# Paired score products on two row groups, with decode and scaling moved between engines, in a fused attention and feed-forward kernel

## The chip, the cores and the metric

The kernel runs on one core of one Trainium2 chip. The metric is the device time of one execution in microseconds; the median of the runs counts.

## The reference, cut to what matters

Windowed attention with a linear bias per head, then two feed-forward blocks over the same 2304 tokens. Sizes: 4 batches, 8 heads, 576 positions, head size 64, window 128.

```python
scores = scale * np.matmul(q, k.transpose(0, 1, 3, 2))
mask = (rel >= 0) & (rel < window)
scores = np.where(mask, scores + bias[None], -1000000000.0)
attn = np.exp(scores - np.max(scores, axis=-1, keepdims=True))
attn = attn / (np.sum(attn, axis=-1, keepdims=True) + 1e-09)
x = np.matmul(attn, v)                     # (B, H, S, D), reshaped to (2304, 512)
h = x @ w_in                               # (2304, 2048)
g = s * np.maximum(h, 0.0) ** 2 + b
x = g @ w_out                              # (2304, 512)
out = ((x @ w1) * (x @ w2)) @ w3 @ w_out2  # the second block
```

The six weight matrices arrive as eight-byte floats; the kernel turns them into single precision itself ("decode").

## The kernel before, in words

The 2304 tokens are cut into six tiles of 384 (`TT`), each of three blocks of 128 queries. A block looks at its own 128 keys and the 128 before them. Attention goes tile by tile, head by head: the heads of tile 0 come first and alone, the heads of tile t+1 are laid between the chunks of the feed-forward work of tile t. A time-line simulation at build time orders each engine's instructions; those passed to `keep_in_program_order` stay in the order in which the code issues them.

The change is about tile 0, whose eight heads (`EARLY`, g = 0 to 7) form four pairs. I call this part the front. Two heads of a pair share one q tile and one k tile, head 0 on partitions 0 to 63, head 1 on 64 to 127. Each call of `slot(n, ...)` (line 1099) for n = 0 to 7 issues for its head:

- `att_scores` (294): first `keep_active` (76), products of zeros that are not used: ten ahead of head 0, two ahead of each other head. Then three products (305), one for each query block, with 64 contracted rows, into two PSUM tiles of the pool `ps_rot`.
- `att_min` (314): VectorE adds the distance table to the three blocks and takes the minimum of each row (324).
- `att_transpose` and `att_select` of the head before: TensorE transposes five 128x128 blocks (380), ScalarE copies them out (394, 395).
- `att_exp` (336): ScalarE, three exponentials (341).
- `tick` (202), as often as `dec` says, for n = 0 to 7: 1, 1, 2, 1, 2, 2, 1, 0 times. A tick starts one decode of a 128x512 weight chunk and finishes the one before. `decode` (89) starts with z on ScalarE (102): the upper half of each number, strided by two, times 2^-112. The rest is VectorE: a shift of z (104), and two operations that combine z and the raw chunk (107, 113). The tile z has two buffers. Raw chunks are loaded on SP's queue (84), three ahead of need.
- `att_v` (409) and `att_x` (446) of the head two before: TensorE multiplies by V with a column of ones (420). After the second head of a pair VectorE forms 1/(sum+1e-9) (452, 455) and multiplies the whole 128x384 product by it (457). TensorE transposes that (462), and `att_xt` (474) copies it out on ScalarE (480). This is a quarter of the input `xT` of tile 0's first product `hp` (505).

After n = 7, `flush` (1082) does what is left of heads 6 and 7. Then slots n = 8 on lay tile 1's heads (310, 311, 272, 257, 347) between the chunks of tile 0's feed-forward block (`hp` 505, `acc` 560), and the decodes go on there.

Of the kernel before, what the change touches and what calls it, by code (L numbers as in the profile page):

```python
# [8 lines left out]
F32 = mybir.dt.float32  # L9
# [3 lines left out]
AF = mybir.ActivationFunctionType  # L13
ALU = mybir.AluOpType

B, H, S, D = 4, 8, 576, 64
# [5 lines left out]
P = 128  # L22
TT = 384
NTILE = NT // TT
NB = TT // P
# [7 lines left out]
EARLY = H  # L33
# [7 lines left out]
def kernel(  # L41
    ctx: ExitStack, tc: tile.TileContext, qk0, qk, v, relm, w_in, w_out, s, b, w1, w2, w3T, wo2, v0, out
):
    nc = tc.nc
# [9 lines left out]
    ps_acc = ctx.enter_context(tc.tile_pool(name="ps_acc", bufs=4, space=PSUM))  # L54
# [21 lines left out]
    def keep_active(dst, n):  # L76
        for _ in range(n):
            nc.tensor.matmul(
                out=dst, lhsT=zeros[:, :P], rhs=zeros[:, :dst.free_size()], start=True, stop=True
            )  # L80
# [8 lines left out]
    def decode(raw, pool, tag, done, free=None, plain=False):  # L89

        z = zp.tile([P, DM], F32, tag="z", name="z")
        pin = tc.keep_in_program_order if pinned[0] else lambda i: i
        if raw.dtype == F32:
            nc.vector.tensor_copy(out=z, in_=raw)
            yield
        else:
            zu = z.bitcast(U32)
            wu = raw.bitcast(U32).rearrange("p (n t) -> p n t", t=2)  # L100
            wf = raw.bitcast(F32).rearrange("p (n t) -> p n t", t=2)
            pin(nc.scalar.activation(out=z, in_=wf[:, :, 1], func=AF.Copy, scale=2.0 ** -112))
            yield
            pin(nc.vector.tensor_scalar(
                out=zu, in0=zu, scalar1=3, scalar2=None, op0=ALU.logical_shift_left
            ))
            pin(nc.vector.scalar_tensor_tensor(
                out=zu, in0=wu[:, :, 1], scalar=0x80000000, in1=zu,
                op0=ALU.bitwise_and, op1=ALU.bitwise_or,
            ))  # L110
            if plain:
                z = pool.tile([P, DM], F32, tag=tag, name="wz")
            nc.vector.scalar_tensor_tensor(
                out=z.bitcast(U32), in0=wu[:, :, 0], scalar=29, in1=zu,
                op0=ALU.logical_shift_right, op1=ALU.bitwise_or,
            )
            if plain:
                done(z)
                yield
                return  # L120
        if free:
            free()
        yield
        w = pool.tile([P, 2, DM], F32R, tag=tag, name="w")
        nc.scalar.activation(out=w[:, 0, :], in_=z, func=AF.Copy)
        nc.gpsimd.tensor_tensor(
            out=w[:, 1, :], in0=z, in1=w[:, 0, :].bitcast(F32), op=ALU.subtract
        )
        done(w)
        yield  # L130
# [59 lines left out]
                    npre[0] += 1  # L190
                    next(p[1])

    pinned = [False]
    flight, todo, keep, raws, nraw, need = [], [], [True], [], [0], [0]

    def load_raws(n):
# [17 lines left out]
    qkraw, vraw, qa, ka, kb, vv, ns, pr, mins, sums, tps, pt, xf, xT, xo = ({} for _ in range(15))  # L214
# [77 lines left out]
        vv[g // 2] = x  # L292

    def att_scores(g):
        a, k, kl = qa.pop(g), ka.pop(g), kb.pop(g, None)
        s0 = ps_rot.tile([P, 2, 2 * P], F32, tag="rot", name="s0")
        s1 = ps_rot.tile([P, 2, 2 * P], F32, tag="rot", name="s1")
        dst = [s0[:, 0, :], s0[:, 1, :], s1[:, 0, :]]
        if g < EARLY:
            keep_active(s0.rearrange("p n q -> p (n q)"), 2 if g else 10)  # L300
        for i in range(NB):
            qs, ks = slice(i * P, (i + 1) * P), slice(i * P, (i + 2) * P)
            if g < EARLY:
                hs, c0 = slice(g % 2 * D, (g % 2 + 1) * D), P if i == 0 else 0
                nc.tensor.matmul(
                    out=dst[i][:, c0:], lhsT=a[hs, qs], rhs=k[hs, i * P + c0:(i + 2) * P],
                    start=True, stop=True,
                )
                continue
            nc.tensor.matmul(out=dst[i], lhsT=a[:, qs], rhs=k[:, ks], start=True, stop=False)  # L310
            nc.tensor.matmul(out=dst[i], lhsT=a[:, qs], rhs=kl[:, ks], start=False, stop=True)  # L311
        ns[g] = dst

    def att_min(g):
        t, h = divmod(g, H)
# [129 lines left out]
    def att_x(g):  # L445
        t, h = divmod(g, H)
        p, e = divmod(g, 2)
        if g < EARLY:
            if e:
                acc = xo.pop(p)  # L450
                rs = ep.tile([P, NB, 2, 1], F32, tag="sm", name="rs")
                nc.vector.tensor_scalar(
                    out=rs, in0=acc[:, :, :, D:], scalar1=1e-9, scalar2=None, op0=ALU.add
                )
                nc.vector.reciprocal(out=rs, in_=rs)
                xs = ap.tile([P, NB, 2, D], F32, tag="cs", name="xs")
                nc.vector.tensor_tensor(
                    out=xs, in0=acc[:, :, :, :D], in1=rs.to_broadcast([P, NB, 2, D]), op=ALU.mult
                )
                xf[p] = ps_acc.tile([P, TT], F32, tag="acc", name="xt")  # L460
                for i in range(NB):
                    nc.tensor.transpose(
                        xf[p][:, i * P:(i + 1) * P], xs[:, i].rearrange("p e d -> p (e d)"), ident
                    )
            return
        pv = tps.pop((g, 0))
        if e == 0:
            xf[p] = ap.tile([P, TT], F32, tag="xf", name="xf")
        main, corr = (slice(0, D), slice(D, P)) if e == 0 else (slice(D, P), slice(0, D))
        cs = ap.tile([P, TT], F32, tag="cs", name="cs")  # L470
        nc.scalar.activation(out=cs[main, :], in_=pv[corr, :], func=AF.Copy)
        nc.vector.tensor_tensor(out=xf[p][main, :], in0=pv[main, :], in1=cs[main, :], op=ALU.add)
# [582 lines left out]
    for c in range(NC1):  # L1055
        for d, src in ((wi, w_in[c]), (wo, w_out[c * P:(c + 1) * P, :])):
            raw = wp.tile([P, DM], src.dtype, tag="w", name="raw")
            raws.append((raw, src))
            todo.append(
                lambda raw=raw, d=d, c=c: decode(  # L1060
                    raw, wp, "w", lambda w: d.__setitem__(c, w), plain=True
                )
            )
# [18 lines left out]
    def flush(g):  # L1082

        att_transpose(g)
        att_select(g)
        for x in (g - 1, g):
            att_split_v(x)
            att_v(x)
            att_x(x)
            att_xt(x)  # L1090
        flushed.update((("T", g), ("V", g - 1), ("V", g)))
# [7 lines left out]
    def slot(n, q, k=2, extra=None, dec=(1, 1)):  # L1099
# [17 lines left out]
        if s1:  # L1117
            splits(n)
            att_scores(n)
            if n + 1 != EARLY:  # L1120
                splits(n + 1)
# [24 lines left out]
        if k == 2:  # L1146
            mlp_h(*seq[2])
        elif v2 is not None:
            att_v(v2)
            att_x(v2)  # L1150
# [7 lines left out]
        if k == 2:  # L1158
            mlp_g(*seq[2])
            if v2 is not None:  # L1160
                att_v(v2)
                att_x(v2)
            mlp_gl(*seq[2])
# [16 lines left out]
            att_load(6)  # L1180
    flush(EARLY - 1)
    q = 0
    pinned[0] = True
    for n, k in enumerate((2, 1, 2, 1, 2, 2, 1, 2, 1, 2), EARLY):
        slot(n, q, k, dec=(k + (n == EARLY + 2), 1))
        q += k
# [152 lines left out]
```

## Time and profile before

| | us |
|---|---|
| median of 3 runs | 846.22 |
| the three runs | 845.83, 846.22, 865.41 |
| the profiled execution, own time | 845.45 |
| its span, from first to last instruction | 843.7 |
| TensorE busy, share of the span | 99% |
| VectorE, ScalarE, GpSimd busy | 76%, 62%, 39% |

The profile gives times in microseconds from the start of the span. PE is TensorE's matmul, PEld its weight load, DVE VectorE, ACT ScalarE, POOL GpSimd, and SPq the queue that issues the transfers. A busy time of PE holds overlapping matmuls, and the row of a merged stretch gives its start, its length, how many instructions it holds (x6), and in brackets what the engine waited for.

### The profile page before, as it was taken

The page shows a single profiled execution, that of the slowest core. Times are in us where ns is not written, and L with a number is a line of the kernel's source. Part 1 is how long each engine was busy: PE and PEld are TensorE (multiplying, and loading weights), DVE is VectorE, ACT ScalarE, POOL GpSimd, SP SyncE. Part 2 cuts the span into 40 slices and gives each one's busy share as a digit, 9 for nine tenths or more (in the row PEclk, how much of TensorE's full clock was granted, in tenths as well). Part 3 has the DMA queues.
Part 4 walks back from the last instruction along what each step waited for, and adds up shares of the span by engine and source line. Part 5 has one row for each costly group of instructions (what it writes and reads, how often), then busy time and mean ns, then how long its engine had stood idle before and what let it go on. Part 6 is the DMA issues. An engine that isn't in the chain of part 4 may idle for free.

```text
span 843.7 us, 14121 instructions
## 1 busy us (share of the span) xinstructions
PE 836.2 (99%) x4746; PEld 780.9 (93%) x4748; DVE 639.6 (76%) x1313; ACT 525.2 (62%) x1242; POOL 332.3 (39%) x346
## 2 busy tenths in 40 slices
PE   8999999999999999999999999999999999999998
PEld 5766667999999999999999999889999999999998
DVE  6989997777778898779774797874989476844485
ACT  7777769887767787777665676334546343632253
POOL 0235457788666776667654300393420000000000
PEclk9999999999999999999999999999999999999999
DMA  9855513112444455444532668964896668756002
GB/s 339 322 175 215 202 55 109 57 57 64 137 139 172 158 173 192 166 158 157 169 110 93 218 248 280 389 247 145 266 315 242 220 245 280 304 169 225 1 1 75
DMA packets 59256, 153.77 MB, mean 182 GB/s; under 512 B 6832, under 2 KB 25520, under 8 KB 59184
## 3 DMA queue, kind: packets, MB, share of 16 engines
q1 hardware_dynamic: 59184, 152.88, 52.2%
q8 instruction: 37, 0.61, 0.3%
q14 instruction: 35, 0.29, 0.1%
HBM read 113.53 MB, written 39.32 MB: 181 GB/s over the span
## 4 chain that ended last, share of the span: by engine, by line
PE 94%; ACT 2%; DVE 2%; DMA 1%; issue 1%; SPq 0%; POOL 0%; ACTq 0%
PE acc L566 20%; PE hp L514 20%; PE u L889 9%; PE e L889 6%; PE w3a L601 5%; PE ou L972 4%; PE acc L560 4%; PE hp L505 4%; PE pv L440 4%; PE oe L972 3%; PE f L889 3%; PE d L889 3%; PE s L310 2%; PE s L311 2%; PE od L972 1%; PE of L972 1%
## 5 line engine op out<-in xcount | busy, mean ns | idle before, releaser
L514 PE MATMUL hp<-x,w 128*128 128x384 f32 x960 | 185.1, 339 | 0.0
L514 PEld LDWEIGHTS hp<-x,w 128*128 128x128 f32 x960 | 167.3, 188 | 0.3
L566 PE MATMUL acc<-gh,w 128*128 128x384 f32 x640 | 125.9, 338 | 0.0
L566 PEld LDWEIGHTS acc<-gh,w 128*128 128x128 f32 x640 | 109.1, 188 | 0.2
L403 POOL TENSOR_SCALAR_AFFINE_SELECT pt<-pp 128x768 fp32r<-128x768 f32 x80 | 79.1, 1011 | 31.6 <-PE pv L440 16.9
L889 PE MATMUL u<-xb,wblk 128*128 128x384 f32 x432 | 83.2, 334 | 0.0
L272 POOL TENSOR_TENSOR kb<-qkraw,ka 128x512 fp32r<-128x512 f32 x40 | 57.4, 1435 | 55.6 <-ACT ka L271 55.3
L889 PEld LDWEIGHTS u<-xb,wblk 128*128 128x128 f32 x432 | 75.6, 188 | 0.3 <-DMA xb<-xfd_T 0.2
L324 DVE CUSTOM_DVE_ANT_0 ns<-s,relm_sb 128x256 f32<-128x256 f32 (+1 forms) x144 | 53.2, 412 | 28.6 <-PE s L311 21.9
L368 POOL TENSOR_SCALAR pr<-pr,sm 128x128 f32<-128x128 f32 x90 | 45.6, 521 | 64.5 <-DVE sm L366 21.0
L566 PE MATMUL acc<-gl,w 128*128 128x384 f32 x320 | 69.6, 337 | 0.0
L898 ACT ACTIVATE p<-u 128x384 f32<-128x384 f32 x48 | 23.6, 491 | 73.4 <-PE u L889 73.4
L543 DVE TENSOR_TENSOR gl<-r,gh 128x384 fp32r<-128x384 f32 x80 | 56.9, 712 | 14.3 <-ACT gh L535 13.1
L525 ACT ACTIVATE r<-hp 128x384 f32<-128x384 f32 x96 | 46.6, 485 | 29.3 <-PE hp L514 27.7
L347 ACT ACTIVATE pr<-pr,mn 128x128 f32<-128x128 f32 x120 | 46.9, 392 | 19.4 <-DVE pr L333 19.1
L889 PE MATMUL e<-xb,wblk 128*128 128x384 f32 x288 | 57.6, 334 | 0.0
L566 PEld LDWEIGHTS acc<-gl,w 128*128 128x128 f32 x320 | 56.6, 188 | 0.0
L654 DVE TENSOR_TENSOR pf<-p,pf 128x384 fp32r<-128x384 f32 x84 | 44.2, 554 | 14.7 <-ACT pf L653 14.2
L653 ACT ACTIVATE pf<-p 128x384 fp32r<-128x384 f32 x84 | 41.7, 522 | 20.3 <-PE ou L972 3.8
L530 ACT ACTIVATE r<-r 128x384 f32<-128x384 f32 x96 | 49.7, 519 | 1.6
L889 PEld LDWEIGHTS e<-xb,wblk 128*128 128x128 f32 x288 | 50.6, 188 | 0.0
L560 PE MATMUL acc<-r,wz 128*128 128x386 f32 x128 | 44.8, 490 | 0.4 <-ACT r L530 0.4
(146 smaller groups left out, 1822.6 us busy)
## 6 DMA issues: line engine op xcount, KB each, us to landing
qkraw<-qk SPq DMA_DIRECT2D x40, 448.0 KB, 3.3
late<-st SPq DMA_DIRECT2D x24, 512.0 KB, 3.4
w<-late SPq DMA_DIRECT2D x24, 512.0 KB, 6.9
wblk<-wfd_S SPq DMA_DIRECT2D x22, 512.0 KB, 5.9
raw<-w_in SPq DMA_DIRECT2D x16, 512.0 KB, 6.5
raw<-w_out SPq DMA_DIRECT2D x16, 512.0 KB, 6.3
st<-w3T SPq DMA_DIRECT2D x16, 512.0 KB, 4.0
wr<-w SPq DMA_DIRECT2D x16, 512.0 KB, 5.4
```

The source lines that it names most:

```text
L272: nc.gpsimd.tensor_tensor(out=kl, in0=k_r, in1=k.bitcast(F32), op=ALU.subtract)
L324: nc.vector.tensor_tensor_reduce(out=n[:, i, cs], in0=dst[i][:, cs], in1=relm_sb[:, VARIANT.get(t * NB + i, 0), cs], scale=2.0 ** -(h + 1) ...
L347: nc.scalar.activation(out=e[:, i, :], in_=e[:, i, :], func=AF.Exp, scale=-1.0, bias=mn[:, i:i + 1], accum_out=sm[:, i:i + 1],)
L403: nc.gpsimd.affine_select(out=o[:, :, :, e, :], in_=pp.bitcast(F32), pattern=[[0, 2], [0, NB], [sign, P]], compare_op=op, fill=0.0, base=0 ...
L514: nc.tensor.matmul(out=hp, lhsT=wi[c][:, l, k * P:(k + 1) * P], rhs=xT[t, k][:, r, :], start=(n == 0), stop=(n == 3 * KD - 1),)
L525: chain(t * NC1 + c, nc.scalar.activation(out=rt[:, :TT], in_=hps.pop((t, c)), func=AF.Relu))
L530: chain(t * NC1 + c, nc.scalar.activation(out=rt[:, :TT], in_=rt[:, :TT], func=AF.Square))
L543: nc.vector.tensor_tensor(out=gl, in0=rt[:, :TT], in1=gh.bitcast(F32), op=ALU.subtract)
L560: nc.tensor.matmul(out=x2acc[m], lhsT=wo[c][:, ms], rhs=g, start=(c == 0), stop=(c == NC1 - 1),)
L566: nc.tensor.matmul(out=x2acc[m], lhsT=wo[c][:, l, ms], rhs=g[r], start=(c == 0 and n == 0), stop=(c == NC1 - 1 and n == 2),)
L889: tc.keep_in_program_order(nc.tensor.matmul(out=dst, lhsT=w[:, l, ks], rhs=xblk[bnm, k][:, r, :], start=(start and n == 0), stop=(n == 5), ...
L972: tc.keep_in_program_order(nc.tensor.matmul(out=dst[m], lhsT=w[:, l, ms], rhs=ys[i][:, r, :], start=(start and i == 0 and k == 0), stop=(i ...
```

## The change

Four edits, all for tile 0:

1. `att_scores` is done once for a pair, at its even head: six products that alternate between the two heads, so between partitions 0 to 63 and 64 to 127, held in that order. The odd head's scores go into two new tiles of the pool `ps_acc`. The call for the odd head returns at once.
2. The zeros stand ahead of head 0 only (ten); the two ahead of each other head are gone.
3. While `front` is true, up to and with `flush`, z is made by GpSimd, not ScalarE. Ten ticks fall into that time.
4. The scaling by 1/(sum+1e-9) is six ScalarE activations of 128x64 for each pair, not one VectorE multiplication of 128x384.

```diff
@@ decode
-            pin(nc.scalar.activation(out=z, in_=wf[:, :, 1], func=AF.Copy, scale=2.0 ** -112))
+            if front[0]:
+                nc.gpsimd.tensor_scalar(
+                    out=z, in0=wf[:, :, 1], scalar1=2.0 ** -112, scalar2=1.0,
+                    op0=ALU.mult, op1=ALU.mult,
+                )
+            else:
+                pin(nc.scalar.activation(out=z, in_=wf[:, :, 1], func=AF.Copy, scale=2.0 ** -112))
...
-    pinned = [False]
+    pinned, front = [False], [True]
@@ att_scores
+        if g in ns:
+            return
         a, k, kl = qa.pop(g), ka.pop(g), kb.pop(g, None)
...
+        ns[g] = dst
         if g < EARLY:
-            keep_active(s0.rearrange("p n q -> p (n q)"), 2 if g else 10)
+            keep_active(s0.rearrange("p n q -> p (n q)"), 0 if g else 10)
+            s2 = ps_acc.tile([P, 2, 2 * P], F32, tag="acc", name="s2")
+            s3 = ps_acc.tile([P, 2, 2 * P], F32, tag="acc", name="s3")
+            ns[g + 1] = [s2[:, 0, :], s2[:, 1, :], s3[:, 0, :]]
+            for i in range(NB):
+                c0 = 0 if i else P
+                for e in range(2):
+                    hs = slice(e * D, (e + 1) * D)
+                    tc.keep_in_program_order(nc.tensor.matmul(
+                        out=ns[g + e][i][:, c0:], lhsT=a[hs, i * P:(i + 1) * P],
+                        rhs=k[hs, i * P + c0:(i + 2) * P], start=True, stop=True,
+                    ))
+            return
         for i in range(NB):
             qs, ks = slice(i * P, (i + 1) * P), slice(i * P, (i + 2) * P)
-            if g < EARLY:
-                hs, c0 = slice(g % 2 * D, (g % 2 + 1) * D), P if i == 0 else 0
-                nc.tensor.matmul(
-                    out=dst[i][:, c0:], lhsT=a[hs, qs], rhs=k[hs, i * P + c0:(i + 2) * P],
-                    start=True, stop=True,
-                )
-                continue
...
-        ns[g] = dst
@@ att_x
-                nc.vector.tensor_tensor(
-                    out=xs, in0=acc[:, :, :, :D], in1=rs.to_broadcast([P, NB, 2, D]), op=ALU.mult
-                )
+                for i in range(NB):
+                    for h in range(2):
+                        nc.scalar.activation(
+                            out=xs[:, i, h, :], in_=acc[:, i, h, :D], func=AF.Copy,
+                            scale=rs[:, i, h, :],
+                        )
@@ after flush(EARLY - 1)
-    pinned[0] = True
+    pinned[0], front[0] = True, False
```

## Rows read from the trace of the kernel before

**Rows 1.** Busy time by stretch: PE, PEld, DVE, ACT, POOL, granted clock, DMA share, GB/s.

```profile
5.27:17.30 12.03, 11.11 (x65) 7.87 (x66) 9.66 (x35) 8.89 (x22) 0.00 (x0) 1.00 0.99 381
17.30:33.60 16.30, 15.93 (x104) 11.60 (x104) 14.96 (x48) 14.51 (x37) 2.94 (x2) 1.00 0.95 372
33.60:44.30 10.70, 10.16 (x57) 7.48 (x56) 8.10 (x25) 6.24 (x19) 2.70 (x3) 1.00 0.71 234
44.30:110.00 65.70, 65.70 (x267) 43.22 (x268) 60.88 (x134) 51.37 (x133) 27.57 (x25) 1.00 0.54 190
```

**Rows 2.** Chain that ended last, pieces of 27 to 45 us: start, length, what.

```profile
30.73 2.18 PE xo L420 x20
...
41.11 1.94 PE hp L505 x6
```

**Rows 3.** Groups of VectorE's instructions, 8.5 to 41 us, by shape.

```profile
L324 DVE CUSTOM_DVE_ANT_0 ns<-s,relm_sb 128x256 f32<-128x256 f32 x17 | 6.9, 419 | 0.2 <-PE s L305 0.2
...
L457 DVE TENSOR_TENSOR xs<-xo,rs 128x384 f32<-128x384 f32 x4 | 2.2, 555 | 0.0
```

**Rows 4.** Timeline of VectorE, 7 to 20.4 us: start, length, instruction, idle before it.

```profile
7.13 0.08 DVE L324 DVE_READ_ACCUMULATOR2_ANT mn<- 128x1 f32 x1
8.51 0.43 DVE L104 TENSOR_SCALAR z<-z 128x512 uint32<-128x512 uint32 x1 [1.30 <-ACT z L102]
...
18.92 0.29 DVE L324 CUSTOM_DVE_ANT_0 ns<-s,relm_sb 128x128 f32<-128x128 f32 x1 [0.75 <-ACT ns L341]
...
19.48 0.55 DVE L457 TENSOR_TENSOR xs<-xo,rs 128x384 f32<-128x384 f32 x1
19.95 0.42 DVE L324 CUSTOM_DVE_ANT_0 ns<-s,relm_sb 128x256 f32<-128x256 f32 x1
...
20.29 0.42 DVE L104 TENSOR_SCALAR z<-z 128x512 uint32<-128x512 uint32 x1
```

**Rows 5.** TensorE: timeline of 5 to 8 us, and the zeros' group, 5.2 to 44.3.

```profile
5.27 1.35 PE L305 MATMUL s<-qkraw,qe 64*128 64x128 f32 x6
6.56 0.60 PE L78 MATMUL s<-zeros 128*128 128x512 bf16 x2
7.09 1.35 PE L305 MATMUL s<-qkraw,qe 64*128 64x128 f32 x6
...
L78 PE MATMUL s<-zeros 128*128 128x512 bf16 x13 | 4.1, 381 | 0.4 <-DVE mn L324 0.4
```

**Rows 6.** Timeline of ScalarE, 7.8 to 11 us.

```profile
7.82 0.67 ACT L102 ACTIVATE z<-raw 128x512 f32<-128x512 f32 x1 [3.06 <-DMA raw<-w_in]
8.38 1.18 ACT L341 ACTIVATE ns<-ns,mn 128x128 f32<-128x128 f32 x3
...
10.69 0.38 ACT L395 ACTIVATE oe<-te 128x256 f32<-128x256 f32 x1
10.95 0.51 ACT L341 ACTIVATE ns<-ns,mn 128x256 f32<-128x256 f32 x1
```

**Rows 7.** GpSimd's prices (ns min/median/max; group), and timeline rows of GpSimd beside VectorE.

```profile
L368 POOL TENSOR_SCALAR pr<-pr,sm x48: 368/376/832, 144.2 to 299.3; 128x128 f32<-128x128 f32 x48
...
L403 POOL TENSOR_SCALAR_AFFINE_SELECT pt<-pp 128x768 fp32r<-128x768 f32 x80 | 79.1, 1011 | 31.6 <-PE pv L440 16.9 <-DVE pp L400 14.6
...
37.01 1.28 POOL L272 TENSOR_TENSOR kb<-qkraw,ka 128x512 fp32r<-128x512 f32 x1 [6.16 <-ACT ka L271]
37.52 0.42 DVE L324 CUSTOM_DVE_ANT_0 ns<-s,relm_sb 128x256 f32<-128x256 f32 x1
...
57.13 1.45 POOL L272 TENSOR_TENSOR kb<-qkraw,ka 128x512 fp32r<-128x512 f32 x1 [3.92 <-ACT ka L271]
57.36 1.64 DVE L333 TENSOR_TENSOR pr<-ns 128x384 f32<-128x384 f32 x1
```

**Rows 8.** The third chunk's load: SP's timeline, and its transfer, us to landing.

```profile
11.50 0.33 SPq L84 DMA_DIRECT2D raw<-w_in  x1
...
raw<-w_in SPq DMA_DIRECT2D x1, 512.0 KB, 6.5
```

## The prediction

> **What bounds the kernel now.** I read the busy times by stretch first, then the chain of waits, then each engine's timeline of the first 45 us. From 44.3 us on TensorE is busy without a gap (65.70 of 65.70 up to 110 us) at a granted clock of 1.00 [rows 1]. What comes after that point is work the change leaves alone, so the whole change is worth what it takes from, or adds to, the time at which TensorE gets there. The chain says when that is: from 30.73 on it holds TensorE's own products, from xo of the last heads to hp at 41.11 [rows 2]. Everything that can be won lies ahead of some 30 us.
>
> In that front three engines are close to full at once. From 5.27 to 17.30 VectorE is busy for 9.66 of 12.03 us, ScalarE 8.89; from 17.30 to 33.60 it is 14.96 and 14.51 of 16.30; GpSimd does nothing in the first stretch and 2.94 in the second [rows 1]. TensorE shows 11.11 and 15.93, but part of that is filler: 13 products of zeros after the first ten [rows 5]. VectorE's gaps are few; two matter, 1.30 us ahead of 8.51 and 0.75 ahead of 18.92 [rows 4]. So the front is set by VectorE's sum of work, with ScalarE next and TensorE behind both. A price taken from TensorE buys little there, a price taken from VectorE buys nearly all of itself.
>
> **Part by part.**
>
> *TensorE.* The zeros: two hold the engine from 6.56 to the next scores at 7.09, 0.27 each; 13 of them are 3.4 us [rows 5]. The scores: the six products behind the first zeros take 1.29 us from their first start to the next instruction's (5.27 to 6.56) [rows 5]; TensorE's records split one single-precision product into two, so six are one head. No row has two row groups next to each other, so the gain of alternating them is bounded by nothing (eight times 1.29, as now) and by full overlap (half of that, 5.2 us off). I take the full overlap, since the two halves share neither rows nor a PSUM tile; but as TensorE is not the bound ahead of 30 us, its 3.4 to 8.6 us turn into idle time, and I enter them as 0. If TensorE were the bound, this is what would be won on top.
>
> What does reach the bound is the order: the odd head's scores lie ready 1.29 us or more earlier. VectorE ends head 0's minima at 7.13 + 0.08 and then idles 1.30 us for the first decode [rows 4], while head 1's scores run from 7.09 to 8.44 [rows 5]. With both heads done by about 6.6 to 7.9, head 1's minima (one of 0.22 and two of 0.35 by starts, some 0.9 together, from [rows 3, 4]) fall into that gap: -0.9. The gap of 0.75 ahead of 18.92 is also ahead of a head's minima, but the row blames an exponential, not scores. Between 0 and 0.75 I take 0.4: -0.4.
>
> *VectorE's scaling goes to ScalarE.* Four multiplications of 0.555 [rows 3]; one costs VectorE 0.47 from its start to the next (19.48 to 19.95) [rows 4]: 4 x 0.47 = -1.9. Against it ScalarE gets 24 small activations. The nearest rows are a copy of 256 columns out of PSUM that cost 0.26 from start to start (10.69 to 10.95), and three exponentials of 128 columns in 1.18, so about 0.36 each [rows 6]. I take 0.25 for 64 columns: 24 x 0.25 = 6.0 (bounds 0.17, as a copy with nothing but its fixed part might cost, and 0.36: 4.1 to 8.6). It loses ten z at 0.56 from start to start (7.82 to 8.38) [rows 6]: 5.6. Net +0.4, bounds -1.5 and +3.0, in front of 12.03 + 16.30 + 10.70 us in which ScalarE is busy for 29.64 of 39.03 [rows 1]. It is hidden at the value I take. What it costs if that cover is gone: the last pair's scaling takes six activations (1.5) in place of 0.55, so x of heads 6 and 7 comes 1 us later; TensorE has hp work in that place (1.94 us at 41.11) [rows 2].
>
> *z goes to GpSimd.* An operation with one input, 512 columns and two multiplications has no row. Its kind with 128 columns takes 0.376; an affine select goes through 768 columns in 1.011, 1.3 ns each [rows 7]. 0.376 + 384 x 1.3 ns = 0.88 us. Bounds: 0.38 (as for 128 columns) and 1.28 (two inputs, 512 columns, at 37.01) [rows 7]. As a step of its own this is 0.2 more than ScalarE's 0.67, one chunk ahead of need, and costs nothing. What it costs is VectorE's time. At 57.36 a VectorE operation with both inputs in SBUF took 1.64 us, where the same kind takes 0.555, beside GpSimd's 1.45 that began at 57.13: it waited until GpSimd was through. The minima at 37.52 have one input in PSUM, lay inside GpSimd's 1.28 from 37.01, and took their usual 0.42 [rows 7]. So each z holds back a combining step of a decode (107, 113) if it falls on one, and no minima.
>
> The Trainium skill, "SBUF — State Buffer", section "Who interferes with whom", states that as an exclusive lock held for the whole instruction, and counts VectorE's `tensor_scalar` from SBUF among those that take it, so the shift (104) too. By that the third of each decode's three steps that I leave free is not free; the sum below would be 3 x 0.43 = 1.3 higher. The rows above agree on operations with two SBUF inputs.
>
> How often? A z can start when the decode two before has freed its z tile, that is at the end of line 113. If minima come next on VectorE (0.9 us) they cover it. If another decode comes next, its shift (0.43) [rows 4] covers half and the rest is waited for. Three of the eight slots finish two decodes in a row (n = 2, 4, 5), so 3 x (0.88 - 0.43) = +1.4. Bounds: 0, and ten times 0.88 = +8.8.
>
> *Transfers.* The loads are not touched, but they stand close: the third chunk's load is issued at 11.50 and lands 6.5 later, at 18.0 [rows 8]; with a z of 0.88 VectorE can shift it at 18.9, and does so now at 20.29 [rows 4]. At that place no more than 1.4 us can be won. My terms up to there (0.9, 0.4, 0.47, less port waits) stay just inside.
>
> **Sum.** -0.9 - 0.4 - 1.9 + 1.4 = -1.8 us. The profiled execution's own time is 845.45 (span 843.7), so 843.65; the median of the runs is 0.77 above that execution, so the forecast is 844.4 us for the median.
>
> **The rivals.**
>
> *GpSimd's hold on the port decides (slower).* If every z falls on a decode's step, at up to 0.88 a piece, VectorE loses 8.8 and wins 3.2: +5.6; with half of it +1.2. It is the other sign from the point at which the ten z cost more than 0.32 us each on the average. For it: decodes are half of VectorE's front, and in the build's order their steps are mixed with minima one by one. Against it: the minima do not wait, and loads that land late spread the z. Time: 847 to 852, at 0.6 a piece 846.2 + 2.8 = 849.
>
> *TensorE falls to the lower clock (slower).* The granted clock is 1.00 in all stretches of the front [rows 1], with zeros between the heads. Without them, and with scores in half the time, TensorE is left with 11.11 + 15.93 - 3.4 - 5.2 = 18.4 us of work in the 28.3 between 5.27 and 33.60, in bursts. If half of that work went at 1.2 in place of 2.4 GHz, it would take 9.2 us more; 9.9 are idle by then, so spread evenly it costs nothing and with half of it on the path +4.6: 849 for the median less what VectorE wins, 851 without. For it: only this edit removes activity. Against it: no idle stretch of TensorE would be longer than a head's minima and exponentials, about 2 us, and transposes and products with V go on.
>
> *No change.* What VectorE gains is eaten by transfers (1.4 us is all there is at 19 us) or by ScalarE, whose last scaling is late: 845.5 to 847.
>
> *The alternation does not overlap.* Then TensorE keeps 5.2 us of score time. It still loses 3.4 of zeros and still has the odd head's scores early, by less (they end at about 7.9): the 0.9 shrinks to about 0.4. Time 844.9. The Trainium skill, "TensorEngine Tiling (Array Packing)", section "Key Properties", says that tiles of the array work independently, and in the same section that a change of the tiling mode drains the engine; by the second, four changes in place of eight are left. No row here shows either.
>
> **How the numbers follow.** Forecast, front shorter by 0.7 to 3.5 (842.7 to 845.5): 0.47, and with it the case without overlap, 0.06. No change (845.5 to 847): 0.20. Port: 0.17. Clock: 0.08. A shorter front by more than 3.5, where TensorE was more of a bound than I think: 0.02. The likeliest case's own range is 842.5 to 845.5. For eight in ten I go down to 841 and up to 849, which takes in half of the port's case. 2% is 17 us, about what a measurement of this kernel can tell from no change. No case above reaches that: faster 0.01, same 0.97, slower 0.02, the last for a clock that stays low past the front.
>
> **What would show it.** Right: the zeros' group is gone after 5.3 us; the odd head's scores start within some ns of the even head's; no VectorE gap ahead of 8.5 us; the gapless stretch of TensorE starts near 42.5 in place of 44.3; z on GpSimd at 0.8 to 0.9 us; rows of lines 107 and 113 with more than 1 us at about three places in the front. Wrong: ten such rows (port); a granted clock under 1.00 between 5 and 35 us, or score products that take twice as long (clock); gaps of VectorE that end with a load (transfers); or a change of several us after 110 us, which would mean that the build's order moved elsewhere.

## The result and the profile after

The changed kernel takes 855.92 us (median of 5 runs, 854.67 to 856.55) against 846.22 for the kernel before: a ratio of 1.0114, 95% interval 1.0103 to 1.0126. It is slower by 9.7 us, where 844.4 was forecast and 841 to 849 was the range. Executions more than 1.5% above the fastest of their kernel, such as 865.41 and 867.04 of the kernel before, stay out of every ratio, and out of the median of o_zero1 below, one of whose four took 1195.66 us. The profiled execution has a span of 854.5 us, 10.8 longer than before.

The first view of after is the busy time by stretch, in the columns and the stretches of [rows 1]:

```profile
5.27:17.30 12.03, 8.29 (x52) 5.86 (x50) 8.66 (x29) 6.14 (x15) 2.69 (x4) 0.86 0.99 378
17.30:33.60 16.30, 8.99 (x56) 6.85 (x55) 14.29 (x37) 9.56 (x27) 6.88 (x8) 0.89 0.90 338
33.60:44.30 10.70, 7.74 (x50) 5.92 (x50) 5.44 (x22) 5.86 (x18) 0.78 (x1) 0.70 0.26 94
44.30:110.00 65.70, 65.16 (x276) 43.44 (x276) 56.34 (x124) 51.14 (x141) 26.34 (x24) 1.00 0.59 205
```

Two things differ from [rows 1]. TensorE's granted clock, 1.00 in every stretch before, is 0.86, 0.89 and 0.70 in the front: a mixture of the two levels, 2.4 and 1.2 GHz. And TensorE is busy for 25.0 of the front's 39.03 us, where it was 37.2. From 44.3 us on the rows nearly agree again.

Where the time went shows in TensorE's timeline of after (start, length, line, tiles, records, idle time before and what ended it):

```profile
5.76 1.44 PE L317 MATMUL s<-qkraw,qe 64*128 64x128 f32 x12
...
11.13 0.44 PE L393 MATMUL te<-ident,ns 128*128 128x128 f32 x2 [2.65 <-ACT ns L354]
...
17.21 1.44 PE L433 MATMUL xo<-vraw,oe 128*128 128x65 f32 x10
22.11 1.24 PE L478 MATMUL xt<-ident,xs 128*128 128x128 f32 x3 [3.47 <-ACT xs L472]
23.28 2.51 PE L317 MATMUL s<-kx,qe 64*128 64x128 f32 x12
25.72 1.10 PE L393 MATMUL te<-ident,ns 128*128 128x128 f32 x5
26.66 1.23 PE L433 MATMUL xo<-vraw,oe 128*128 128x65 f32 x10
...
28.64 1.33 PE L433 MATMUL xo<-vraw,oe 128*128 128x65 f32 x10
36.56 1.29 PE L478 MATMUL xt<-ident,xs 128*128 128x128 f32 x3 [6.58 <-ACT xs L472]
37.78 2.48 PE L317 MATMUL s<-kx,qe 64*128 64x128 f32 x12
40.19 0.77 PE L393 MATMUL te<-ident,ns 128*128 128x128 f32 x5
...
44.32 1.56 PE L521 MATMUL hp<-xe,wz 128*128 128x384 f32 x4
...
54.96 0.39 PE L324 MATMUL s<-ka,qa 128*128 128x256 f32 x1 [0.54 <-DVE mn L337]
```

The last row is a landmark. The same score product of tile 1, with the same wait of 0.54 us, stands in the trace of before at 44.27:

```profile
44.27 0.39 PE L310 MATMUL s<-ka,qa 128*128 128x256 f32 x1 [0.54 <-DVE mn L324]
```

It is 10.69 us late, nearly the whole difference of the spans (10.8), so next to nothing is lost or won behind it. Ahead of it TensorE twice waits for the scaled x of a pair, 3.47 and 6.58 us, because the next pair's held scores stand behind that pair's transposes. A third wait, 2.65 us at 11.13, is for exponentials whose minima stand on VectorE behind the shift of the first decode, which itself waited 1.76 us for z, up to 9.77. And the held scores, twelve records in 1.44 us at 5.76, take 2.51 at 23.28: the lower level of the clock.

The longest wait is not the scaling's own length. TensorE is through with that pair's products at 29.97 (28.64 + 1.33). VectorE, busy with minima and with the steps of decodes, begins rs for it only at 35.49, and ScalarE's six activations follow:

```profile
35.49 0.16 DVE L465 TENSOR_SCALAR rs<-xo 128x6 f32<-128x6 f32 x1
35.98 1.34 ACT L472 ACTIVATE xs<-xo,rs 128x64 f32<-128x64 f32 x6 [3.00 <-DVE rs L468]
```

An estimate from the two traces says how much is waiting and how much is clock. On the way to the first hp (33.68 before, 44.32 after) TensorE waits 13.7 us, where it waited 0.9. By stretches of 1 us it is busy for some 10 us at the lower level, which stretches its work by some 5. It is spared the 3.4 and 5.2 us that the prediction counted. 12.8 + 5 - 8.6 = 9.2, of 10.6 that hp is late. So in the changed kernel the waits weigh more than the clock; how much of the waiting the slower products caused, these rows do not say.

### The profile page after: what moved, and what is told of

It reads as the page before. It is cut to its first block, busy times and chain, and to the rows that moved or that the text cites. A ratio compares the mean times of both kernels' runs of the same rounds, so it can differ in the third digit from the quotient of the medians.

```text
span 854.5 us, 14131 instructions
## 1 busy us (share of the span) xinstructions
PE 834.1 (98%) x4734; PEld 780.3 (91%) x4734; DVE 637.4 (75%) x1309; ACT 525.8 (62%) x1256; POOL 339.8 (40%) x356
## 4 chain that ended last, share of the span: by engine, by line
PE 91%; DVE 3%; ACT 2%; DMA 2%; issue 1%; POOL 0%; SPq 0%; ACTq 0%; DVEq 0%
PE acc L582 20%; PE hp L530 20%; PE u L905 9%; PE e L905 6%; PE w3a L617 5%; PE ou L988 4%; PE acc L576 4%; PE hp L521 4%; PE pv L453 4%; PE oe L988 3%; PE f L905 3%; PE d L905 3%; PE s L324 2%; PE s L325 2%; PE od L988 1%; PE of L988 1%
## 5 line engine op out<-in xcount | busy, mean ns | idle before, releaser
L559 DVE TENSOR_TENSOR gl<-r,gh 128x384 fp32r<-128x384 f32 x80 | 56.1, 702 | 14.4 <-ACT gh L551 13.1
L294 POOL TENSOR_TENSOR vv<-vraw,vv 128x256 fp32r<-128x256 f32 x40 | 40.2, 1024 | 15.3 <-ACT vv L292 15.2
```

Source lines behind the costliest of these rows:

```text
L559: nc.vector.tensor_tensor(out=gl, in0=rt[:, :TT], in1=gh.bitcast(F32), op=ALU.subtract)
```

## The experiments

All times are medians; the kernel before took 845.5 to 846.2 us beside them. The theories: **Clock** (the zeros kept TensorE at 2.4 GHz; without them its small products run at half speed and set the front), **Order** (the held score order makes TensorE wait for the scaling), **Port** (z on GpSimd holds VectorE back), **Scaling** (ScalarE's activations are late). The edits are against the kernel after (u_, f_) or before (o_), unless another is named.

**One part undone at a time.** *u_pin*, the scores not held in order:

```
-                    tc.keep_in_program_order(nc.tensor.matmul(
+                    nc.tensor.matmul(
```

> The changed kernel, with the twelve score records of a pair no longer held in program order. Theory Order (in the changed kernel TensorE's scores of pairs 2 and 3 stand behind the transposes xt of pairs 0 and 1, which wait for the scaling: 3.3 and 6.0 us of waiting): the even heads' scores go ahead of xt, at least half of the 9.3 us comes back, 846 to 851. Theory Clock (without zeros TensorE runs at its lower level, 0.70 to 0.89 granted between 5 and 44 us): nothing about the zeros changes, 854 to 857. Theory GpSimd (z comes late and holds VectorE's port): nothing changes, 854 to 857.

*u_zero*, four products of zeros ahead of each later pair:

```
-            keep_active(s0.rearrange("p n q -> p (n q)"), 0 if g else 10)
+            keep_active(s0.rearrange("p n q -> p (n q)"), 4 if g else 10)
```

> The changed kernel, with four zero products ahead of each later pair again (as many in all as before). Theory Clock: granted clock back to 1.00 through the front and 847 to 850. Theory Order: the clock alone is worth 1 to 2 us, as TensorE's products on the path between 22 and 44 us are some 8 us of which a quarter to a half were stretched; 853 to 855. Theory GpSimd: 854 to 857.

*u_z*, z back on ScalarE:

```
-    pinned, front = [False], [True]
+    pinned, front = [False], [False]
```

> The changed kernel, with z made by ScalarE as before (no GpSimd in the decode). Theory GpSimd: no late z and no port waits, 846 to 850. Theory Order: xt still stands ahead of the scores and waits for the scaling; less on VectorE ahead of it, 1 to 3 us better, 852 to 855. Theory Clock: 854 to 857.

*u_xs*, the scaling back on VectorE:

```
-                for i in range(NB):
-                    for h in range(2):
-                        nc.scalar.activation(
...
+                nc.vector.tensor_tensor(
+                    out=xs, in0=acc[:, :, :, :D], in1=rs.to_broadcast([P, NB, 2, D]), op=ALU.mult
+                )
```

> The changed kernel, with the scaling of P.V on VectorE again (one operation of 128x384 for a pair). Theory Scaling (six activations of 1.34 us in all are late on ScalarE): 846 to 851. Theory Order: the scaling is on the waited-for path twice, so 0.8 us shorter each time, 853 to 855. Theories Clock and GpSimd: 854 to 857.

Measured: u_pin 852.87 (ratio 1.0093, 1.0073 to 1.0113), u_zero 855.23 (1.0107, 1.0080 to 1.0133), u_z 853.64 (1.0095, 1.0079 to 1.0110), u_xs 855.68 (1.0113, 1.0096 to 1.0130). No single part brings back more than 3.1 us of the 9.7. The trace of u_pin says why (its profiled execution took 856.11 us, the other three 852.61 to 853.01). Its front by stretch, columns as above:

```profile
17.30:33.60 16.30, 15.19 (x62) 11.23 (x61) 12.63 (x42) 10.20 (x29) 6.50 (x7) 0.65 0.90 342
33.60:44.30 10.70, 10.37 (x40) 8.77 (x41) 5.59 (x16) 6.07 (x20) 1.03 (x1) 0.50 0.22 76
```

And a piece of its TensorE timeline:

```profile
34.76 2.50 PE L317 MATMUL s<-kx,qe 64*128 64x128 f32 x6
37.19 0.69 PE L478 MATMUL xt<-ident,xs 128*128 128x128 f32 x2
37.67 3.52 PE L433 MATMUL xo<-vraw,oe 128*128 128x65 f32 x16
...
43.23 2.12 PE L521 MATMUL hp<-xe,wz 128*128 128x384 f32 x3
```

The waits for xs are gone, TensorE is almost without a gap, and it is no less slow: all of the second stretch runs at 0.50. Six score records take 2.50 us, where six took 1.35 in [rows 5], and sixteen products with V take 3.52, where twenty took 2.18 in [rows 2]. The clock is back (0.99) only in the stretch from 44.3 us on, where the products of 384 columns (hp) stand; they begin at 43.23. What Order loses by waiting, the clock takes in its place. u_z lands where Order put it (852 to 855), with a clock of 0.72, 0.92 and 0.81 in the three stretches. u_zero and u_xs keep the held order and its waits (4.5 and 10.1 us ahead of the transposes of xs), and their granted clock from 33.6 to 44.3 us is 0.50 too.

**One part done at a time.** *o_zero*, the kernel before with nothing changed but its later zeros left out:

```
-            keep_active(s0.rearrange("p n q -> p (n q)"), 2 if g else 10)
+            keep_active(s0.rearrange("p n q -> p (n q)"), 0 if g else 10)
```

> The kernel before, with the zeros ahead of heads 1 to 7 left out and nothing else. Theory Clock: the granted clock falls in the front and the time is 849 to 856. Theory Order: nothing of the order changes, 845 to 847, or 844 to 845 by the 3.4 us of TensorE that zeros took if TensorE bounds the front.

*o_zero1* leaves one zero product of the two:

```
+            keep_active(s0.rearrange("p n q -> p (n q)"), 1 if g else 10)
```

> The kernel before with one zero product ahead of each later head, not two. Theory Clock: between the kernel before (1.00, 846) and none (0.50 from 17 to 44 us, 860): the granted clock falls in part of the front, 849 to 857. Theory Order, or zeros as mere filler: 844.5 to 846, 0.27 us saved for each of seven.

*o_pair*, the paired, alternating, held scores alone (the change's `att_scores`, with four zeros ahead of each later pair, as many as two heads had):

```
+            keep_active(s0.rearrange("p n q -> p (n q)"), 4 if g else 10)
```

> The kernel before with the paired, alternating, ordered scores alone (four zeros ahead of each later pair, decode and scaling as before). Theory Order: TensorE waits for xt of the pair two before, by 3 to 6 us in all: 848 to 852, with the clock falling after such a wait. Theory Clock without order: zeros stand, 845 to 847. My prediction's own terms: 844.9, by the odd head's earlier minima.

*o_z*, z by GpSimd alone (with `front`, as in the change):

```
-            pin(nc.scalar.activation(out=z, in_=wf[:, :, 1], func=AF.Copy, scale=2.0 ** -112))
+            if front[0]:
+                nc.gpsimd.tensor_scalar(
...
```

> The kernel before with z by GpSimd alone. Theory GpSimd: VectorE waits for the port and z comes late, 848 to 852. Theories Clock and Order: zeros and order as before, 845 to 847; my prediction's term for it was +1.4 us.

*o_xs*, the scaling by ScalarE alone:

```
-                nc.vector.tensor_tensor(
-                    out=xs, in0=acc[:, :, :, :D], in1=rs.to_broadcast([P, NB, 2, D]), op=ALU.mult
-                )
+                for i in range(NB):
+                    for h in range(2):
+                        nc.scalar.activation(
...
```

> The kernel before with the scaling of P.V by ScalarE alone (six activations for a pair). Theory Scaling: ScalarE is behind, 847 to 850. Theories Clock and Order: zeros and order stay, 845 to 847; my prediction's terms: 0.4 to 1.9 us less than before.

*u_pinzero*, the kernel after with u_pin's and u_zero's edits together:

> The changed kernel with both of these undone at once: the score products free in the order, and four zero products ahead of each later pair. Each alone gave back 1 to 3 of 9.7 us. Theory Both (each alone leaves the other: with the order freed TensorE has no waits left but runs at half clock from 23 to 44 us; with zeros it waits 4.5 us for the scaling and falls to half clock afterwards): together 845 to 848. Theory Clock alone, with more zeros needed than four for a pair: granted clock still under 0.9 in 17 to 44 us, 849 to 853. Theory GpSimd or Scaling (the moved work costs the rest): TensorE at full clock, yet 850 or more.

Measured: o_zero 860.39 (1.0175, 1.0141 to 1.0208), o_zero1 861.93 (1.0191, 1.0168 to 1.0215), o_pair 856.45 (1.0120, 1.0099 to 1.0141), o_z 847.17 (1.0023, 0.9993 to 1.0053), o_xs 850.88 (1.0053, 1.0033 to 1.0072), u_pinzero 853.83 (1.0098, 1.0080 to 1.0116).

Alone, then, leaving out the zeros costs 14.4 us, the held pairs, with the zeros only ahead of even heads, 10.5, the scaling on ScalarE 5.1 and z on GpSimd 1.2, the last with an interval that holds no change. u_pinzero undoes two parts at once and still takes 853.83: its clock is 1.00 up to 17.3 us, but at 30.02 TensorE waits 1.46 us for exponentials, and from 33.6 to 44.3 us the clock is 0.53. Four zeros ahead of each pair do not hold it, even with no order held.

o_zero is the plainest run of all. It removes work (14 products of zeros) and moves none between engines, and it costs more than the whole change. Its stretches:

```profile
5.27:17.30 12.03, 9.56 (x45) 6.69 (x44) 9.45 (x30) 8.08 (x19) 0.00 (x0) 0.83 0.92 361
17.30:33.60 16.30, 16.30 (x64) 13.40 (x63) 13.78 (x40) 11.50 (x26) 2.75 (x2) 0.50 0.79 311
33.60:44.30 10.70, 10.70 (x41) 8.90 (x42) 4.38 (x18) 4.77 (x12) 0.00 (x0) 0.50 0.36 117
```

The rows of its TensorE timeline where the clock falls:

```profile
8.93 1.19 PE L380 MATMUL te<-ident,ns 128*128 128x128 f32 x5 [1.23 <-ACT ns L341]
11.31 1.33 PE L420 MATMUL xo<-vraw,oe 128*128 128x65 f32 x10 [1.18 <-ACT oe L394]
12.57 1.94 PE L305 MATMUL s<-qkraw,qe 64*128 64x128 f32 x6
14.44 1.33 PE L380 MATMUL te<-ident,ns 128*128 128x128 f32 x5
15.70 2.50 PE L305 MATMUL s<-qkraw,qe 64*128 64x128 f32 x6
```

The five transposes at 13.30 in the trace of before:

```profile
13.30 0.76 PE L380 MATMUL te<-ident,ns 128*128 128x128 f32 x5
```

Two waits of 1.2 us, and from about 13 us on every product takes twice its time: the same six score records 1.94, then 2.50, the five transposes 1.33 in place of 0.76. TensorE has no gap from 17.3 to 44.3 us, and the clock stays at 0.50 all that time. A busy engine is not enough, then: here the front's own transposes, 64-row scores and 65-column products did not bring the clock back. In after such products did, three times, each time within some 4 us from the start of twelve alternating scores (half speed at 23.28, full at 26.66). Nor is that sure: in u_xs the clock stays at 0.50 behind twelve of them at 36.85, to the end of the front. Which work brings the clock back no run isolates. What o_zero shows is Clock, and with no other part of the change beside it.

The Trainium skill, "TensorE: Matmul & The Clock Gate", section "HAM oscillation — how this bites in real kernels", puts the fall down to waits between short bursts of products, each of which then starts at the lower rate. The trace agrees that the fall comes behind waits, though these (1.23 and 1.18 us) are shorter than those of the page, and goes beyond it: 27.0 us without a wait at 0.50.

o_pair and o_xs fall by the same path. o_pair has the held order's wait, 2.79 us at 33.04, and then a clock of 0.50 in 33.6 to 44.3. o_xs keeps its clock at 1.00 up to 17.3 us, and has 0.86 and 0.74 in the next two stretches; its TensorE timeline shows where a head's minima come late:

```profile
26.82 0.55 PE L380 MATMUL te<-ident,ns 128*128 128x128 f32 x3
28.73 0.52 PE L380 MATMUL te<-ident,ns 128*128 128x128 f32 x2 [1.36 <-DVE mn L324]
29.05 1.06 PE L78 MATMUL s<-zeros 128*128 128x512 bf16 x2
30.04 2.50 PE L305 MATMUL s<-kx,qe 64*128 64x128 f32 x6
```

Within one kernel the time follows the mean granted clock from execution to execution as well: f_pin2 (below) took 849.56 to 850.05 us at 0.993 or 0.994, and 853.11 to 854.86 at 0.990. o_z keeps 1.00 in its profile, but three of its ten executions had 0.992 to 0.994 and took 850.61 to 853.72. Port alone is worth some 1.2 us, if anything. And one execution of the kernel before beside it took 852.41 at 0.992: its own zeros hold the clock in most executions, not in all.

**More zeros.** *f_pin2* gives every later head its two zeros again, the odd heads in a PSUM tile of their own; *f_free4* gives four, with the scores not held:

```
         if g in ns:
+            zt = ps_rot.tile([P, 2, 2 * P], F32, tag="rot", name="zt")
+            keep_active(zt.rearrange("p n q -> p (n q)"), 2)
             return
...
+            keep_active(s0.rearrange("p n q -> p (n q)"), 2 if g else 10)
```

> The changed kernel with two zero products ahead of every later head's slot again, so two also in the odd head's slot, into a PSUM tile of their own; the scores stay paired, alternating and in held order. Theory Clock (what counts is that zeros stand in every head's slot, not their number for a pair): granted clock near 1.00 up to 44 us and 846 to 849. Theory Order (TensorE waits for xt of the pair two before, whatever the clock): waits of 3 to 5 us remain, and 849 to 853 with a clock that falls after each wait.

> The changed kernel with its scores free in the order and four zero products in every later head's slot, even and odd: neither a held order nor a lack of zeros is left. If clock and order are all there is: granted clock 1.00 through the front, 844 to 848. If the paired scores themselves cost more (the odd head's scores late because their PSUM tiles are shared with P.V and its transposes): full clock and 849 or more.

Measured: f_pin2 851.58 (1.0072, 1.0048 to 1.0096), f_free4 851.78 (1.0067, 1.0039 to 1.0095). Some 4 us of the loss are gone. The clock is not held yet. In the profile of f_free4 (an execution of 854.19 us; three of the six kept 0.998 and took 848.15 to 851.15) it is 0.64 in 33.6 to 44.3 us: at 30.23 the zeros themselves wait 2.20 us for a head's minima, which read tiles of the same PSUM pool. In f_pin2 it is 0.69 in 17.3 to 33.6, after a wait of 1.77 for xs, and 1.00 behind that. And the waits ahead of te (1.86 us in f_pin2, 1.21 in f_free4) have no zeros just before them.

**Zeros where the waits are.** Four kernels with two more products of zeros ahead of each head's transposes: *g_pin* (f_pin2 with them), *g_free* (the same, scores not held), *g_oxs* (o_xs with them), and *g_old*, the kernel before with nothing but them:

```
                 tp = ps_rot.tile([P, n, P], F32, tag="rot", name="te")
+                if not b0:
+                    keep_active(tp.rearrange("p n q -> p (n q)"), 2)
```

> The changed kernel with two products of zeros in every later head's slot and two more ahead of each head's transposes; scores held in order. Clock theory (the lower clock is the whole loss): granted clock 1.00 from 5 to 44 us, median 845 to 847. Order theory (TensorE waits behind the scaling in the held order, and this costs by itself): clock 1.00 but waits of 3 us or more ahead of the transposes of xs, median 849 to 851. If the zeros do not hold the clock (under 0.9 in a stretch): 850 to 853.

> The same zeros as in g_pin, scores not held in order. Clock theory: clock 1.00, 844.5 to 846.5. Order theory: 2 us or more below g_pin. If holding the order has no price at full clock: within 1 us of g_pin.

> The kernel before, the scaling on ScalarE, and two products of zeros ahead of each head's transposes. Scaling on ScalarE without these zeros took 850.9, with a granted clock of 0.86 and 0.74 in two stretches. Clock theory: these zeros cover the wait ahead of te, clock 1.00, and the median is 845 to 847. Rival (six activations in place of one multiplication lengthen the path of the last pair by themselves): 849 to 851 at a clock of 1.00.

> The kernel before with the two products of zeros ahead of each head's transposes alone. 16 products of 0.27 us. If TensorE has room ahead of 30 us: 846 to 847. If it is the bound there: up to 4.3 us more, 850.

Measured: g_pin 852.72 (1.0070, 1.0045 to 1.0096), g_free 847.52 (1.0011, 0.9989 to 1.0032), g_oxs 850.36 (1.0041, 1.0016 to 1.0065), g_old 848.27 (1.0024, 1.0010 to 1.0039). The stretches of g_free:

```profile
5.27:17.30 12.03, 10.32 (x74) 7.18 (x73) 9.75 (x34) 7.16 (x18) 2.74 (x4) 1.00 0.96 365
17.30:33.60 16.30, 15.35 (x97) 11.01 (x95) 14.65 (x44) 12.16 (x38) 7.59 (x8) 1.00 0.98 386
33.60:44.30 10.70, 10.70 (x68) 8.38 (x67) 8.24 (x25) 8.22 (x30) 3.11 (x4) 1.00 0.64 219
```

With the clock at 1.00 in all three stretches of this execution (three of the ten had 0.997 over the span), the change as a whole (paired scores, z on GpSimd, scaling on ScalarE) is no longer slower by an amount that can be told from none. Against g_old, which has the same zeros ahead of its transposes, it is 0.75 us faster by the medians, with overlapping intervals. g_old's own stretches:

```profile
5.27:17.30 12.03, 11.47 (x60) 7.01 (x60) 9.13 (x32) 8.52 (x20) 0.00 (x0) 1.00 1.01 384
17.30:33.60 16.30, 16.30 (x112) 12.34 (x111) 15.00 (x49) 13.95 (x35) 2.55 (x2) 1.00 0.96 369
33.60:44.30 10.70, 10.70 (x67) 8.38 (x66) 9.15 (x26) 6.99 (x20) 3.28 (x3) 1.00 0.65 228
```

g_old also prices TensorE's time. Two of its added zeros take 0.44 us to the next start (13.83 to 14.27), so 16 are 3.5 us, and they cost 2.1 (0.8 to 3.3 by the interval). More than half of what TensorE is given in the front comes out at the end, and with it TensorE has no gap from 17.3 us on: in the kernel before it was close to the bound there.

g_pin misses Clock's number. The zeros didn't hold the clock in it (0.86 in the first stretch, behind a wait of 2.50 us ahead of te), and a wait of 2.87 us for xs is left at 30.46. So the held order costs 5.2 us against g_free, by waits and the clock together; what it would cost at 1.00 throughout no run shows. g_oxs held its clock at 1.00 and still took 2.1 us more than g_old, but the two intervals overlap: Scaling's own price, 0 to some 3 us, is left open.

**Which zeros, and z again.** *h_te* is g_free without the zeros at the scores and in the odd heads' slots (16 of 30 are left, all ahead of te). *h_z* is g_free with z on ScalarE (the edit of u_z).

```
-            zt = ps_rot.tile([P, 2, 2 * P], F32, tag="rot", name="zt")
-            keep_active(zt.rearrange("p n q -> p (n q)"), 2)
...
+            keep_active(s0.rearrange("p n q -> p (n q)"), 0 if g else 10)
```

> g_free without its zeros ahead of later scores and in the odd heads' slots: 14 products of 0.27 us fewer, 16 left, all ahead of the transposes. If two a head hold the clock at 1.00: TensorE's front is up to 3.8 us shorter, of which g_old gave back about half, so 845 to 847. If the zeros are needed at every wait: granted clock under 0.95 in a stretch of the front and 849 to 853.

> g_free with z on ScalarE. If z on GpSimd costs VectorE 1.4 us by the port, as the prediction had it, and this reaches the end: 846.1. If TensorE sets the front here: within 0.7 us of 847.5. If ScalarE with both z and the scaling becomes the bound: 848.5 to 850.

Measured: h_te 853.58 (1.0074, 1.0051 to 1.0098), h_z 849.12 (1.0039, 1.0025 to 1.0054). In h_te the clock falls twice. The second time, in stretches of 3 us:

```profile
26.00:29.00 3.00, 2.70 (x16) 1.93 (x17) 2.94 (x3) 1.28 (x3) 2.59 (x2) 1.00 1.04 404
29.00:32.00 3.00, 1.19 (x6) 0.57 (x5) 3.00 (x13) 2.11 (x8) 0.75 (x1) 1.00 1.01 397
32.00:35.00 3.00, 3.00 (x13) 2.20 (x13) 2.96 (x10) 1.93 (x7) 1.04 (x1) 0.63 0.22 88
35.00:38.00 3.00, 3.00 (x16) 3.00 (x16) 1.25 (x2) 1.62 (x5) 0.00 (x0) 0.50 0.45 130
38.00:41.00 3.00, 3.00 (x14) 2.52 (x13) 0.93 (x3) 1.83 (x8) 0.00 (x0) 0.50 0.36 105
```

TensorE is busy for 1.19 of 3 us (a wait of 1.44 us for minima and one of 0.62 for xs), and the clock pays for it over the 9 us behind, in which TensorE never waits. h_z went to the third case of its expectation: with z and the scaling both on ScalarE, that engine is full (3.00 of 3.00 from 8 to 11 us), TensorE waits 1.40 and 1.21 us for exponentials, and the clock is 0.86 in the first stretch. This fits z on GpSimd making room for the scaling there; by the medians the pair is worth having together (847.52 against 849.12), but the intervals of g_free and h_z overlap.

No version beat the kernel before.

## Why the prediction was wrong

**The step that failed** is the one on TensorE: "as TensorE is not the bound ahead of 30 us, its 3.4 to 8.6 us turn into idle time, and I enter them as 0". The idle time was the cost. The zeros were no filler but what held the clock, and without them, with the scores held, TensorE's queue became the path: on the way to the first hp it waits some 12.8 us more than before and is stretched by some 5 at the lower clock. The rival of the clock stood in the text, at a chance of 0.08 and 849 to 851; what happened is that rival and the held order's waits together, at 855.9. Two reasons kept it small, and both fell:

- "no idle stretch of TensorE would be longer than a head's minima and exponentials, about 2 us." Waits of 3.47 and 6.58 us came. I had the odd head's scores ready earlier, and hadn't asked what the held order puts them behind: pair 2's scores now stand behind the transposes of pair 0, which wait for rs on VectorE and then for xs; the order on VectorE, with decode steps ahead of rs, makes most of the longest wait. Nor are long waits needed: o_zero fell after two of 1.2 us.
- "9.9 are idle by then, so spread evenly it costs nothing and with half of it on the path +4.6." The size of the stretch was near (some 5 us in after), but the idle time was no reserve to absorb it: it lay in waits on the path itself. And half of the work was not the most that could be at 1.2 GHz: o_zero had all of it at 0.50 from about 13 us, and u_pin from 23, on to the hp products, with hardly a gap.

The row that should have warned stood in [rows 1]: TensorE busy for 11.11, 15.93 and 10.16 of 12.03, 16.30 and 10.70 us, 95% of the front. I took the zeros off that as slack. g_old shows there was little: it lost 2.1 us for 3.5 us of added zeros.

**Other steps, by their traces.**

- *Alternating row groups* (taken as full overlap): right. Twelve records in 1.36 us at full clock (g_free at 11.36) against six in 1.35 [rows 5]. Only while the order holds them together, though: without it pairs 2 and 3 ran as two groups of six again, and why the odd head's went later there wasn't pursued.
- *Gap ahead of the first decode* (-0.9): right where the load comes on time. It is 0.43 us in g_free (before 1.30 [rows 4]). In after it is 1.76, since the first load landed later there and z began at 9.09; in before ScalarE began it at 7.82 [rows 6].
- *z on GpSimd* (0.88 each): too high. In after the shortest take 0.64 or 0.65 us, the longest 1.03, and the ten 7.5 us in all, 0.75 each.
- *Port waits* (+1.4): right in size, wrong in place. VectorE's groups of the ten decodes in g_free, 5.2 to 44.3 us:

```profile
L119 DVE SCALAR_TENSOR_TENSOR wz<-raw,z 128x512 uint32<-128x512 uint32 x10 | 8.1, 813 | 0.1
L113 DVE SCALAR_TENSOR_TENSOR z<-raw,z 128x512 uint32<-128x512 uint32 x10 | 7.7, 770 | 0.0
L110 DVE TENSOR_SCALAR z<-z 128x512 uint32<-128x512 uint32 x10 | 5.3, 527 | 1.0 <-POOL z L103 1.0
```

Their sum is 21.1 us, and 19.7 in the trace of before (8.1, 7.4 and 4.2): +1.4. Most of it, 1.1, is on the shift (L110; 0.42 us in [rows 4]), which the prediction left free of the port. In after one shift took 1.49, by VectorE's timeline:

```profile
28.31 1.49 DVE L110 TENSOR_SCALAR z<-z 128x512 uint32<-128x512 uint32 x1
```

GpSimd's timeline of after has two instructions beside it, of which the first ends at 29.52:

```profile
27.81 1.71 POOL L278 TENSOR_TENSOR kb<-qkraw,ka 128x512 fp32r<-128x512 f32 x1
29.49 0.81 POOL L103 TENSOR_SCALAR z<-raw 128x512 f32<-128x512 f32 x1
```

The sentence of the Trainium skill's "SBUF — State Buffer", "Who interferes with whom", that counts `tensor_scalar` among those that can take the port fits these rows (the shift at 1.49 in place of 0.42 us) better than my reading did.

- *Scaling on ScalarE* (0.25 each): near. 24 in 5.3 us in g_free, 0.22 each. That the scaling would be hidden was wrong for pairs 0 and 1 in the held order, where TensorE waited for it.
- *The sum* (-1.8 us): with the clock at 1.00 on both sides, g_free against g_old, -0.75, in agreement with a small gain and with none. The -0.4 no run shows by itself; the -1.9 did not reach the end in g_oxs, which is 2.1 us above g_old with TensorE gapless in both from 17.3 us on.

## What to carry to other kernels

Before products of zeros or other "idle" matmuls are taken out, or TensorE's share of a stretch is made smaller, the clock has a price of its own: ask which products the stretch would be left with, and price all of them at half speed until a trace shows the clock back. Here that took 3 to 4 us in after and lasted to the next stretch of large products in o_zero, so the next busy moment is not enough. An order held by hand should be read along the whole queue: for each held instruction, what stands ahead of it there and who ends that one's wait. And when a single undo brings back little, undo in pairs, and read in the trace whether the pair is undone: u_pinzero had both edits and brought back 2.1 us of 9.7, as its clock still fell; g_free, with more zeros and some of them ahead of the transposes, brought back 8.4.

## What the runs showed that was not expected

- Gapless work kept the lower level: 27.0 us in o_zero (17.3 to 44.3), 10.37 busy of 10.70 us in u_pin, all at 0.50. In the stretch from 44.3 on, where the 384-column products are, it was back at 0.98 (o_zero), 0.99 (u_pin) and 1.00 (after). In after it had come back earlier as well, three times, under the front's small products.
- One product of zeros ahead of each head did not hold the clock, two did, with all else equal: 861.93 (o_zero1) and 845.75 us beside it. One was no better than none (860.39, o_zero).
- The placing counts as much as the number: 16 later zeros ahead of te lost the clock (h_te, 853.58); 14 ahead of the scores held it in the kernel before, in its order and with its waits.
